# Hash products of twelve rows, four at once, in a kernel of LSH attention and spatial gating

## The chip, the cores and the metric

One core of one Trainium2 chip runs the whole program. The metric is the device time of one execution in microseconds (us), the median of several runs.

## The reference

Two stages, one behind the other. Attention runs over batch 4, heads 8, sequence 768 and head size 64; a query sees only the keys that fall into its own bucket of a random-projection hash of 6 bits. A gated MLP over the sequence follows, with model size 512 and hidden size 1024.

```
q_bits = einsum('bhsd,dk->bhsk', q, proj) > 0        # k_bits the same; 6 bits
mask   = q_bucket[:, :, :, None] == k_bucket[:, :, None, :]
scores = where(mask, q @ k.T / 8, -1e9);  attn = softmax(scores);  x = attn @ v

h = relu(x @ w_in);  u, v = h[..., :512], h[..., 512:]
v_n = (v - mean(v)) / sqrt(var(v) + 1e-6)
out = (u * (einsum('ts,bsd->btd', w_spatial, v_n) + b_spatial)) @ w_out
```

## The kernel before

**The work.** The 32 heads are taken as 16 pairs (`p`), two heads (`e`) in the lower and upper 64 partitions. Each pair has six score steps (`scores`), one for each block of 128 rows. Inputs are float32; each operand is split into a high and a low float16 part, and a product is made of three: `hl` holds the four parts of a pair's q and k. Four passes (`ALL`) make a step's scores in PSUM: three of `hl`, with 64 rows for each head, and a last one of `hk`, the hash rows. A hash row is a bit, scaled so large (`HQ`, `HK`) that a pair of query and key in different buckets falls out of the softmax. Each pass has four products of 384 columns: two halves `c` of the sequence and two heads `e`. Heads lie in different row groups of TensorE (PE), so the two heads of a pass run side by side.

The hash rows (`hash_rows`) are made by PE (`hp`) and VectorE (DVE: `sg`), and moved by eight small DMAs, 12 rows of 384 numbers each, issued by GpSimd (POOL), from `sg` to their place in `hk`. There are two `hk` tiles in turn; those of pair 1 lie in `ws`, which is free that early. Of `hk`, group 1 is the stationary side of a by-query head and group 0 the moving side.

**Two kinds of heads.** Heads 2, 4, 6 and 8 (`KEYS`, in pairs 1 to 4) have their scores laid out with keys on partitions, which needs the maximum of each row ahead of time: `row_max` computes it, `max_row` turns it on PE (`tp`), copies it on DVE (`mt`) and moves it by a DMA of SyncE's queue (SP) into row 63 of the head's `hk`. All other heads go by queries: DVE takes the maximum and the scores out of PSUM (`low`, `ex`), `bias` scales the maximum (`nb`), ScalarE (ACT) takes the exponential and its float16 part (`exp`, `half`: `pp`), DVE or POOL subtracts to get the rest (`rest`), SP turns the result by a DMA transpose (`turn`: `pt`), and PE multiplies it with v (`weighted`: `pv`), four steps later. After four pairs a batch's MLP units become ready: `vps`, `ups`, `sps` and `ops`, groups of three products that PE takes between the steps.

**What sets the order.** The kernel writes every piece of work down as an operation (`op`) with an engine, an estimated length and a rank. `timetable` then plays the engines through and gives each operation a start; where two engines are allowed ("VG") it takes the one that would be first. The program is issued in the order of these starts, and on the chip each engine goes through its own list in that order. The table `LATER` adds to the rank of operations of one name, the paces `T_FIRST` to `T_LAST` say how far apart score steps are planned, `LATE` and `LATE_D` add a margin before PE uses a result, `R_QK` ranks the loads of q and k, `W_FROM` and `W_EVERY` time the weights' loads, and gaps of PE are filled with small warm products (`warm`).

Of the kernel before, what the change touches and what calls it, by code (L numbers as in the profile page):

```python
# [18 lines left out]
P = 128  # L19
D = 64  # L20
NB = 6
# [14 lines left out]
def lsh_attention_spatial_gating(  # L36
# [15 lines left out]
    HS = S // 2  # L52
# [8 lines left out]
    KEYS = WIDE | set()  # L61
    wide = lambda p: any(2 * p + e in WIDE for e in range(2))
    keys = lambda p: [e for e in range(2) if 2 * p + e in KEYS]
    byq = lambda p: [e for e in range(2) if 2 * p + e not in KEYS]
    const = ctx.enter_context(tc.tile_pool(name="const", bufs=1))
    wk = ctx.enter_context(tc.tile_pool(name="wk", bufs=1))
# [8 lines left out]
    AGAIN = {"P": 0.0, "A": 0.11, "V": 0.11, "G": 0.07, "S": 0.0}  # L75
    X = 0.14
    TURN = 1.92
    LATER = {'relu': 0.1, 'first': -0.9, 'bias': -0.3, 'bits': 0.1, 'stats': 0.2, 'half': -0.1, 'copy': 0.6, 'scale': 0.3, 'newton': -0.4, 'turn': 0.1, 'low': 0.6, 'exp': -0.1, 'factor': -0.3}
    ops = []


# [25 lines left out]
    def op(e, d, fn, *after, on=(), rank=4, land=0.0, dma=0.0, need=None, gives=None, alone=False):  # L107
        later = LATER.get(fn.__name__.strip("<>"), 0.0)
        if not isinstance(rank, tuple):
            rank = rank + later  # L110
        elif rank[1]:
            rank = (rank[0] + later, rank[1])
        o = Op(e, d, fn, rank, land, dma)
        o.need, o.gives, o.alone = need, gives, ("V" if alone or "G" in e else "") + ("G" if fn.__name__ != "move" else "")
        wait = [a for a in after if a is not None]
        for h in on:
            assert not h.closed
            if not h.users:
                wait += h.before
            h.users.append(o)  # L120
        for a in {id(a): a for a in wait}.values():
            a.then.append(o)
            o.left += 1
        return o

    def timetable(free, banks):
# [12 lines left out]
        def key(o):  # L139
            return o.rank if isinstance(o.rank, tuple) else (step[0] + (4 if o.rank > 8 else 0), o.rank)  # L140

        def banked(o, e):


            if not o.need:
                return max(o.ready, port[0] + (0.0 if e == port[1] else 0.02)) if e in o.alone else o.ready
            have = sorted(banks[o.need[0]])
            return max(o.ready, have[o.need[1] - 1]) if len(have) >= o.need[1] else None
# [5 lines left out]
        while open_:  # L154
# [12 lines left out]
            for o in came[e]:  # L167
                r = banked(o, e)
                if r is not None and r <= t0 + LOOK and (pick is None or key(o) < key(pick[0])):
                    if not (o.need and o.need[0] in wants and wants[o.need[0]] < key(o)):  # L170
# [38 lines left out]
        for t, n in fill:  # L209
            op("P", 0.07 * n, lambda n=n: warm(n)).start = t  # L210
# [8 lines left out]
    at = {}  # L219
    tags = {}  # L220

    def buf(name, n):
        if name not in tags:
            tags[name] = Buf(n)
        return tags[name]
# [17 lines left out]
    hk = [const.tile([P, 2, S], F16, name=f"hk{i}") for i in range(2)]  # L243
    hkt = lambda p: hk1 if p == 1 else hk[(p + 1) % 2 if p else 0]
    hk1 = flat[1][:, :2 * S].rearrange("p (g s) -> p g s", g=2)
    for i, t in enumerate(hk + [hk1]):
        eng = nc.vector if i < 2 else nc.gpsimd
# [84 lines left out]
    held = {}  # L332

    def load_qk(p, *after):
# [6 lines left out]

        at["qk", p] = op("S", 0.45, go, *after, on=[h], rank=R_QK, dma=2.95)

    def load_v(p, *after):
# [9 lines left out]

        at["v", p] = op("S", 0.5, go, *after, on=[h], rank=R_QK, dma=1.45)

    def urgent(p):

        return NT * p - (8 if keys(p) else 3)

    def hash_rows(p, *after):
        qk, k = held["qk", p], (buf("hk", 2) if p != 1 else buf("hk1", 1)).new()
        held["hk", p] = k
        g0, g1 = buf("sg0", 1).new(), buf("sg1", 2).new()
        hp, sg = [], []

        def go():
            hp.append(bank_m(f"hp{p}"))
            for j in range(4):
                nc.tensor.matmul(  # L370
                    hp[0][32 * j:32 * j + 32, :HS], lhsT=pj,
                    rhs=st["qk", p][:, 1 - j // 2, (j % 2) * HS:(j % 2 + 1) * HS],
                    start=True, stop=True, tile_position=(0, 32 * j))

        def bits():
            sg.append(wk.tile([P, HS], F16, tag="sg0", name=f"sg0_{p}"))
            nc.vector.tensor_scalar(sg[0], hp[0][:, :HS], 0.0, hv[:, 0:1], op0=ALU.is_gt, op1=ALU.subtract)

        def scale():
            sg.append(wk.tile([P, HS], F16, tag="sg1", bufs=2, name=f"sg1_{p}"))  # L380
            nc.vector.tensor_scalar(sg[1], sg[0], hv[:, 1:2], None, op0=ALU.mult)

        t = op("P", 0.8, go, at["qk", p], *after, on=[qk], rank=(urgent(p), 3), need=("m", 1))
        t = op("V", 0.54, bits, t, on=[g0], rank=(urgent(p), 2), gives="m")
        t = op("V", 0.24, scale, t, on=[g0, g1], rank=(urgent(p), 2), alone=True)
        at["hk", p] = []
        for j in range(4):
            for e in range(2):
                q, eng = HQ_FIRST[e] if p == 0 else HQ_REST

                def move(j=j, e=e, eng=eng):
                    eng.dma_start(  # L392
                        out=hkt(p)[D * e:D * e + 2 * NB, 1 - j // 2, (j % 2) * HS:(j % 2 + 1) * HS],
                        in_=sg[1][32 * j + 16 * e:32 * j + 16 * e + 2 * NB, :])
                at["hk", p].append(op(q, 0.53 if q == "G" else 0.75, move, t, on=[g1, k], rank=(urgent(p), 3), land=2.8 if q == "G" else 1.8))

    def split_qk(p, *after):
        qk, h = held["qk", p], (buf("hl", 2) if p != 1 else buf("hl1", 1)).new()
        held["hl", p] = h

        def high():
            if p == 1:
                st["hl", p] = flat[0][:, :4 * S].rearrange("p (g s) -> p g s", g=4)
            else:
                st["hl", p] = wk.tile([P, 4, S], F16, tag="hl", bufs=2, name=f"hl{p}")
            nc.scalar.activation(st["hl", p][:, 1:3], st["qk", p], AF.Copy, scale=SQ)

        t = op("A", 1.39, high, at["qk", p], *after, on=[qk, h], rank=(urgent(p), 4))
        at["hl", p] = [t] + [
            op("V", 0.88, lambda to=to, part=part, frm=frm: nc.vector.scalar_tensor_tensor(  # L410
                out=st["hl", p][:, to], in0=st["qk", p][:, part], scalar=SQ, in1=st["hl", p][:, frm],
                op0=ALU.mult, op1=ALU.subtract), t, on=[qk, h], rank=(urgent(p), 4), alone=True)
            for to, part, frm in ((0, 1, 2), (3, 0, 1))]
# [64 lines left out]
    def sums(ps, p, rows, passes, queries, halves=(0, 1), heads=(0, 1)):  # L478

        for a, (x, y, last) in enumerate(passes):  # L480
            for c in halves:
                cs = slice(c * HS, (c + 1) * HS)
                for e in heads:
                    byq_ = queries or 2 * p + e not in KEYS
                    r = slice(D * e, D * e + D - (last and byq_))
                    src = hkt(p) if last else st["hl", p]
                    l, m = (x, y) if byq_ else (y, x)
                    nc.tensor.matmul(ps[e][:, c - halves[0]], lhsT=src[r, l, rows], rhs=src[r, m, cs],  # L488
                                     start=(a == 0), stop=(a == len(passes) - 1))

    def scores(p, i, g, begin):
        sc = buf("sc", 1).new()

        def go():
            ps = st["sc", p, i] = [ps_sc.tile([P, 2, 512], F32, tag="sc", name=f"sp{p}_{i}_{e}")[:, :, :HS] for e in range(2)]
            sums(ps, p, slice(i * P, (i + 1) * P), ALL, False)

        t = op("P", 1.42, go, *at["hl", p], *at["hk", p], on=[sc, held["hl", p], held["hk", p]], rank=(g, 0))
        t.ready = begin
        at["S now"] = t  # L500
        for e in range(2):
            (by_keys if 2 * p + e in KEYS else by_queries)(p, i, e, g, t, sc)
# [474 lines left out]

    EB, PB, PTB, XTB, VB, UB = 4, 4, 9, 6, 6, 2
    LAG, LAG0, LAGK = 4, 3, 2
    T_FIRST, T_KEYS, T_QUERIES, T_THIRD, T_LAST = 5.0, 5.4, 5.6, 5.95, 5.75  # L980
    START = 6.5
    LOOK = 0
    R_MAX = 0.05
    R_QK = 0.95
    REST, BIAS = (0.88, 1.6), (0.22, 0.25)
    CROSS = {NP - 1}
    R_W = 0.1
    LATE, LATE_D = 0.3, 2.0
    GAP, WARM = 0.5, 5.0
    AHEAD = 1  # L990
    MANY = 36
    W_FROM, W_EVERY = 21.0, 2.0
    HQ_FIRST = (("S", nc.sync), ("A", nc.scalar))
    HQ_REST = ("G", nc.gpsimd)

# [1 line left out]
    load_qk(0)  # L997
    load_v(0)
    hash_rows(0)
    load_qk(1)  # L1000
    split_qk(0)
# [8 lines left out]
    for g in range(STEPS + LAG):  # L1010
        p, i = divmod(g, NT)
        for e in range(2):
            while todo[e] < STEPS and todo[e] + lag[2 * (todo[e] // NT) + e] <= g:
                m, j = divmod(todo[e], NT)
# [97 lines left out]
```

## Time and profile before

| | |
|---|---|
| median of 3 runs | 663.7 us (663.58 to 666.67) |
| profiled execution | 666.77 us, its span 665.0 us |
| granted TensorE clock | 0.99 |
| PE, DVE, ACT, POOL busy | 625.8, 498.4, 476.3, 257.0 us |
| products of `hk` of pairs 5 to 15 | 264, all from 177.8 us on |
| small DMAs `hk<-sg` issued by POOL | 112, 9.0 KB each |
| DMA transposes `pt<-pp` | 168 |

The span is the time from the first to the last instruction. In rows of groups, the numbers behind the bar are busy time, mean length of one in ns, and idle time of the engine before them with what ended it. In rows of the timeline they are start and length in us, engine, line, operation, output and inputs, and a count. Waits are total, number of times, longest. Products overlap, so starts tell more than lengths.

### The profile page before, as it was taken

Reading aid. Unit: us, or ns where it says so; the run is one execution under the profiler, and the core shown is the slowest. Engines: PE = TensorE matmul, PEld = TensorE weight load, DVE = VectorE, ACT = ScalarE, POOL = GpSimd, SP = SyncE. Lnnn points to the kernel's source line nnn. Section 1 sums busy time; section 2 is a strip of 40 time slices with the busy share of each in tenths; the row PEclk is TensorE's granted clock in tenths of the full one; section 3 lists DMA queues with packets and bytes.
Section 4 is the critical chain, followed back from the end, with each engine's and each line's share of the span. In section 5 each row is a group of like instructions: output and inputs, shape, how many; then the busy total and the mean of one; then the engine's idle time right before and its main releaser. Section 6 shows DMA issues by size and latency. Waiting matters only on the chain.

```text
span 665.0 us, 17570 instructions
## 1 busy us (share of the span) xinstructions
PE 625.8 (94%) x7068; PEld 382.8 (58%) x7068; DVE 498.4 (75%) x1019; ACT 476.3 (72%) x802; POOL 257.0 (39%) x318
## 2 busy tenths in 40 slices
PE   5787999998999999999999999999999999999997
PEld 4364767675645655655555566565555665556553
DVE  6787999899898958777867787888877677365250
ACT  2785667867888998777769986787889977463121
POOL 3491624424665757241526345131426541000000
PEclk9797999999999999999999999999999999999999
DMA  5798888894999899999998999899999988210102
GB/s 182 185 183 201 174 170 171 206 219 110 208 189 201 153 193 224 198 184 226 164 232 146 226 141 211 171 221 183 199 215 153 157 140 154 45 47 1 48 1 95
DMA packets 310274, 108.53 MB, mean 163 GB/s; under 512 B 297265, under 2 KB 300337, under 8 KB 310193
## 3 DMA queue, kind: packets, MB, share of 16 engines
q1 hardware_dynamic: 306256, 106.26, 83.4%
q0 software_dynamic: 3840, 1.12, 0.9%
q8 instruction: 55, 0.90, 0.6%
q14 instruction: 27, 0.21, 0.1%
q10 hardware_dynamic: 96, 0.04, 0.0%
HBM read 27.94 MB, written 6.29 MB: 51 GB/s over the span
## 4 chain that ended last, share of the span: by engine, by line
PE 46%; DMA 10%; DVE 8%; issue 5%; ACT 4%; SPq 0%; POOL 0%; DVEq 0%; POOLq 0%; ACTq 0%
DMA pt<-pp 10%; PE sps L742 9%; PE sp L488 9%; PE ops L742 8%; PE pv L645 7%; PE ups L742 6%; PE vps L742 4%; DVE ex L517 3%; PE vpp L742 2%; ACT ex L527 1%; ACT pp L531 1%; DVE hl L410 1%; DVE pp L535 1%; PE upp L742 1%; DVE vr L820 1%
## 5 line engine op out<-in xcount | busy, mean ns | idle before, releaser
L517 DVE TENSOR_SCALAR_CACHE_REDUCE ex<-sp 128x768 f32<-128x768 f32 x168 | 155.7, 951 | 36.8 <-PE sp L488 36.7
L527 ACT ACTIVATE ex<-ex,nb 128x768 f32<-128x768 f32 x168 | 155.4, 932 | 6.6 <-POOL nb L522 4.0
L535 POOL TENSOR_TENSOR pp<-ex,pp 128x768 f16<-128x768 f32 x63 | 104.0, 1657 | 115.4 <-ACT pp L531 85.5
L531 ACT CAST pp<-ex 128x768 f16<-128x768 f32 x168 | 136.1, 825 | 6.2 <-DMA pt<-pp 5.2
L645 PEld LDWEIGHTS <-pt 128*128 128x128 f16 x3024 | 105.6, 97 | 48.8 <-issue 22.4
L535 DVE TENSOR_TENSOR pp<-ex,pp 128x768 f16<-128x768 f32 x105 | 101.2, 979 | 42.9 <-ACT pp L531 41.7
L645 PE MATMUL pv<-vp,pt 128*128 128x65 f16 x3024 | 118.6, 193 | 7.8 <-DMA pt<-pp 6.6
L488 PE MATMUL sp<-hl 64*128 64x384 f16 x1080 | 110.4, 328 | 8.5 <-DVE ex L517 6.2
L742 PE MATMUL sps<-ws,vn 128*128 128x384 f16 x576 | 101.1, 326 | 0.1
L488 PEld LDWEIGHTS <-hl 64*128 64x128 f16 x1116 | 52.8, 95 | 62.4 <-issue 34.9
L742 PEld LDWEIGHTS <-vn 128*128 128x128 f16 x576 | 53.7, 98 | 35.0 <-issue 2.1
L392 POOL DMA_DIRECT2D hk<-sg x112 | 58.0, 525 | 24.2 <-issue 10.3
L742 PE MATMUL ops<-wo,g 128*128 128x512 f16 x288 | 65.9, 379 | 0.4 <-DVE u L906 0.3
L524 ACT ACTIVATE nb<-mr 128x1 f32<-128x1 f32 x125 | 24.5, 197 | 57.8 <-DVE ex L517 57.1
L742 PE MATMUL ups<-xt,wi 128*128 128x384 f16 x348 | 62.4, 326 | 0.0
L742 PE MATMUL vps<-wi,xt 128*128 128x512 f16 x234 | 57.0, 379 | 0.9 <-ACT vr L825 0.7
L488 PE MATMUL sp<-hk 63*128 63x384 f16 (+1 forms) x360 | 48.6, 327 | 2.8 <-DMA hk<-sg 2.3
L742 PEld LDWEIGHTS <-wi 128*128 128x128 f16 x384 | 35.2, 97 | 22.4 <-issue 1.8
L742 PEld LDWEIGHTS <-g 128*128 128x128 f16 x288 | 26.9, 98 | 30.8 <-issue 1.6
L742 PEld LDWEIGHTS <-xt 128*128 128x128 f16 x288 | 25.5, 97 | 28.2 <-issue 3.9
L932 DVE SCALAR_TENSOR_TENSOR sy<-sps,bt 128x384 f32<-128x384 f32 x32 | 17.8, 557 | 31.0 <-PE sps L742 30.6
L940 ACT CAST g<-sy 128x384 f16<-128x384 f32 x32 | 16.3, 508 | 31.4 <-DVE sy L944 30.4
(112 smaller groups left out, 798.2 us busy)
## 6 DMA issues: line engine op xcount, KB each, us to landing
qk<-kq SPq DMA_DIRECT2D x16, 768.0 KB
out<-o SPq DMA_DIRECT2D x24, 256.0 KB
v<-v SPq DMA_DIRECT2D x12, 384.0 KB
pt<-pp SPq DMA_TRANSPOSE x168
raw<-w_in SPq DMA_DIRECT2D x8, 256.0 KB
raws<-w_in SPq DMA_DIRECT2D x8, 256.0 KB
hk<-sg POOLq DMA_DIRECT2D x112, 9.0 KB, 3.8
vf<-v SPq DMA_DIRECT2D x4, 384.0 KB
```

Source lines behind the costliest of these rows:

```text
L392: eng.dma_start(out=hkt(p)[D * e:D * e + 2 * NB, 1 - j // 2, (j % 2) * HS:(j % 2 + 1) * HS], in_=sg[1][32 * j + 16 * e:32 * j + 16 * e + 2 ...
L410: op("V", 0.88, lambda to=to, part=part, frm=frm: nc.vector.scalar_tensor_tensor(out=st["hl", p][:, to], in0=st["qk", p][:, part], scalar= ...
L488: nc.tensor.matmul(ps[e][:, c - halves[0]], lhsT=src[r, l, rows], rhs=src[r, m, cs], start=(a == 0), stop=(a == len(passes) - 1))
L517: nc.vector.tensor_scalar(ex, st["sc", p, i][e], -float(2 ** 28), None, op0=ALU.max, op1=ALU.max, accum_out=st["mx", n][:, i:i + 1])
L524: nc.scalar.activation(nb, mx, AF.Copy, scale=-ISQ)
L527: nc.scalar.activation(st["e32", n, i], st["e32", n, i], AF.Exp, bias=st["nb", n][:, i:i + 1], scale=ISQ)
L531: nc.scalar.copy(st["pp", n, i][:, 0], st["e32", n, i])
L535: eng.tensor_tensor(out=st["pp", n, i][:, 1], in0=st.pop(("e32", n, i)), in1=st["pp", n, i][:, 0], op=ALU.subtract)
L645: nc.tensor.matmul(o, lhsT=l, rhs=m, start=(i == 0 and k == 0), stop=(i == NT - 1 and k == len(todo_) - 1))
L742: nc.tensor.matmul(c[0], lhsT=l(), rhs=r(), start=(j == 0), stop=(j == len(products) - 1))
L932: nc.vector.scalar_tensor_tensor(out=y[0], in0=c[0], scalar=1.0 / (SN * SW), in1=bt[:, hs], op0=ALU.mult, op1=ALU.add)
L940: nc.scalar.copy(gt[h][0][:, d], y[0])
```

## The change

For the pairs behind the last head by keys (`four`, pairs 5 to 15) the hash rows lie in tiles of 32 rows. The moving side's half `c` goes to rows 32c of its head's 64, and the stationary side is written twice, to rows 0 and to rows 32 (`again`: four more DMAs for each pair). The last pass then takes 12 rows at 64e + 32c, a row group of its own for each of its four products; before, it took 63 rows for each head, most of them without a bit. The step's estimated length goes from 1.42 to 1.32. The paces, ranks and margins are other numbers.

```
+    four = lambda p: p > max(KEYS) // 2
-    LATER = {'relu': 0.1, 'first': -0.9, 'bias': -0.3, 'bits': 0.1, 'stats': 0.2, 'half': -0.1, ... 'turn': 0.1, ...}
+    LATER = {'relu': 0.1, 'first': -0.5, 'bias': -0.3, 'bits': 0.1, 'stats': 0.3, 'half': -0.4, ... 'turn': -0.6, 'rest': -0.1}
...
-                def move(j=j, e=e, eng=eng):
+                def move(j=j, e=e, eng=eng, at=32 * (j % 2) if four(p) and j > 1 else 0):
                     eng.dma_start(
-                        out=hkt(p)[D * e:D * e + 2 * NB, 1 - j // 2, (j % 2) * HS:(j % 2 + 1) * HS],
+                        out=hkt(p)[D * e + at:D * e + at + 2 * NB, 1 - j // 2, (j % 2) * HS:(j % 2 + 1) * HS],
                         in_=sg[1][32 * j + 16 * e:32 * j + 16 * e + 2 * NB, :])
...
+                if four(p) and j < 2:
+                    def again(move=move):
+                        move(at=32)
+
+                    at["hk", p].append(op(q, 0.53, again, t, on=[g1, k], rank=(urgent(p), 3), land=2.8))
...
                     r = slice(D * e, D * e + D - (last and byq_))
+                    if last and four(p):
+                        r = slice(D * e + 32 * c, D * e + 32 * c + 2 * NB)
...
-        t = op("P", 1.42, go, ...)
+        t = op("P", 1.32 if four(p) else 1.42, go, ...)
...
-    T_FIRST, T_KEYS, T_QUERIES, T_THIRD, T_LAST = 5.0, 5.4, 5.6, 5.95, 5.75
+    T_FIRST, T_KEYS, T_QUERIES, T_THIRD, T_LAST = 5.0, 5.4, 5.55, 5.75, 5.95
-    R_QK = 0.95
+    R_QK = 1.25
```

`LOOK` goes from 0 to 0.05, `LATE_D` from 2.0 to 2.25, `W_EVERY` from 2.0 to 2.1. Lines of the changed kernel lie one to eight further down. In the built program POOL issues 156 of the small DMAs instead of 112, 23 of the 168 subtractions `pp` have gone from DVE to POOL (DVE 105 to 82, POOL 63 to 86), as have five of `g` and six of `sy`, and there are 444 warm products instead of 436.

The order, at three places. First SP's queue ahead of pair 1; `pt0_4` and `pt1_4` are the transposes of heads 0 and 1 at step 4, `qk3` is the load of pair 3, `raw` are weights, and `ws1<-mt2` is the max row of head 2 (pair 1). Before:

```order
L539 DMA_TRANSPOSE pt0_4_677<-pp0_4_604 128x12x128
L539 DMA_TRANSPOSE pt1_4_713<-pp1_4_654 128x12x128
L340 DMA qk3_760<-kq 128x1536
L292 DMA raw5_784<-w_in 128x256
L619 DMA ws1_80<-mt2_788 1x6x128
L539 DMA_TRANSPOSE pt0_5_814<-pp0_5_735 128x12x128
```

Now:

```order
L547 DMA_TRANSPOSE pt0_4_663<-pp0_4_611 128x12x128
L547 DMA_TRANSPOSE pt1_4_700<-pp1_4_660 128x12x128
L627 DMA ws1_80<-mt2_742 1x6x128
L293 DMA raw5_789<-w_in 128x256
L341 DMA qk3_796<-kq 128x1536
L293 DMA raws_299<-w_in 128x256
L547 DMA_TRANSPOSE pt0_5_875<-pp0_5_846 128x12x128
```

The max row's DMA has moved ahead of the two loads, one more load stands ahead of step 5's transposes.

Second, PE at the turn of that max row (`tp2`). Before, it stands behind head 1's `pv` group of step 3:

```order
L645 MATMUL pv1_483<-vp0_92,pt1_3_630 128x64
L645 LDWEIGHTS pt1_3_630
L645 MATMUL pv1_483<-vp0_92,pt1_3_630 128x65
L612 LDWEIGHTS m16_2_739
L612 MATMUL tp2_767<-ident_71,m16_2_739 6x128
L216 LDWEIGHTS ident_71
```

Now it stands directly behind pair 0's last score step, ahead of head 1's group of step 2:

```order
L496 LDWEIGHTS hk0_81
L496 MATMUL sp0_5_1_641<-hk0_81 128x384
L620 LDWEIGHTS m16_2_638
L620 MATMUL tp2_665<-ident_71,m16_2_638 6x128
L653 LDWEIGHTS pt1_2_544
L653 MATMUL pv1_483<-vp0_92,pt1_2_544 128x65
```

It has moved ahead of three `pv` groups: head 1 of step 2, head 0 and head 1 of step 3.

Third, POOL around the hash rows of pair 12 (`hk1<-sg1_12`); `pp23_1` is the subtraction of head 23 (pair 11) at step 1, `nb24` and `pp25_0` belong to pair 12. Before:

```order
L522 TENSOR_SCALAR nb22_6685<-mr22_6684 128x1
L884 TENSOR_TENSOR vn1_1_6061<-vr1_5_6300,vn1_0_6060 128x512
L392 DMA hk1_82<-sg1_12_6769 12x384 x8
L687 TENSOR_TENSOR xs10_6883<-x20_6846,xs10_6883 128x6x64
L535 TENSOR_TENSOR pp23_1_6888<-ex23_1_6821,pp23_1_6888 128x768
```

Now:

```order
L543 TENSOR_TENSOR pp23_3_7039<-ex23_3_6990,pp23_3_7039 128x768
L955 TENSOR_TENSOR g1_1_0_6897<-sy1_2_0_7029,g1_0_0_6896 128x384
L952 TENSOR_TENSOR sy1_3_0_7125<-sy1_3_0_7125,u1_0_6306 128x384
L393 DMA hk1_82<-sg1_12_7133 12x384 x12
L530 TENSOR_SCALAR nb24_7380<-mr24_7379 128x1
L543 TENSOR_TENSOR pp25_0_7450<-ex25_0_7394,pp25_0_7450 128x768
```

The DMAs have moved from early in pair 11 to directly ahead of pair 12's first step; those of pair 13 stand alike, and those of pairs 5, 6, 7 and 8 shortly ahead of their pair.

More of the change, by code (lines that the diff above doesn't have):

```diff
@@ L77, in lsh_attention_spatial_gating @@
     TURN = 1.92
-    LATER = {'relu': 0.1, 'first': -0.9, 'bias': -0.3, 'bits': 0.1, 'stats': 0.2, 'half': -0.1, 'copy': 0.6, 'scale': 0.3, 'newton': -0.4, 'turn': 0.1, 'low': 0.6, 'exp': -0.1, 'factor': -0.3}
+    LATER = {'relu': 0.1, 'first': -0.5, 'bias': -0.3, 'bits': 0.1, 'stats': 0.3, 'half': -0.4, 'copy': 0.6, 'scale': 0.3, 'newton': -0.4, 'low': 0.6, 'exp': -0.1, 'factor': -0.3, 'turn': -0.6, 'rest': -0.1}
     ops = []
@@ L113, in op @@
         o = Op(e, d, fn, rank, land, dma)
-        o.need, o.gives, o.alone = need, gives, ("V" if alone or "G" in e else "") + ("G" if fn.__name__ != "move" else "")
+        o.need, o.gives, o.alone = need, gives, ("V" if alone or "G" in e else "") + ("G" if fn.__name__ not in ("move", "again") else "")
         wait = [a for a in after if a is not None]
@@ L496, in go @@
             sums(ps, p, slice(i * P, (i + 1) * P), ALL, False)
-        t = op("P", 1.42, go, *at["hl", p], *at["hk", p], on=[sc, held["hl", p], held["hk", p]], rank=(g, 0))
+        t = op("P", 1.32 if four(p) else 1.42, go, *at["hl", p], *at["hk", p], on=[sc, held["hl", p], held["hk", p]], rank=(g, 0))
         t.ready = begin
@@ L979, in lsh_attention_spatial_gating @@
     LAG, LAG0, LAGK = 4, 3, 2
-    T_FIRST, T_KEYS, T_QUERIES, T_THIRD, T_LAST = 5.0, 5.4, 5.6, 5.95, 5.75
+    T_FIRST, T_KEYS, T_QUERIES, T_THIRD, T_LAST = 5.0, 5.4, 5.55, 5.75, 5.95
     START = 6.5
-    LOOK = 0
+    LOOK = 0.05
     R_MAX = 0.05
-    R_QK = 0.95
+    R_QK = 1.25
     REST, BIAS = (0.88, 1.6), (0.22, 0.25)
@@ L987, in lsh_attention_spatial_gating @@
     R_W = 0.1
-    LATE, LATE_D = 0.3, 2.0
+    LATE, LATE_D = 0.3, 2.25
     GAP, WARM = 0.5, 5.0
@@ L991, in lsh_attention_spatial_gating @@
     MANY = 36
-    W_FROM, W_EVERY = 21.0, 2.0
+    W_FROM, W_EVERY = 21.0, 2.1
     HQ_FIRST = (("S", nc.sync), ("A", nc.scalar))
```

## The prediction

> **What bounds the kernel now.** I read the shares of busy time and the slices first, then the stages, then what TensorE (PE) waits for in each of them, and last single steps on the timeline.
>
> ```profile
> span 665.0 us, 17570 instructions
> PE 625.8 (94%) x7068; PEld 382.8 (58%) x7068; DVE 498.4 (75%) x1019; ACT 476.3 (72%) x802; POOL 257.0 (39%) x318
> ...
> PE   5787999998999999999999999999999999999997
> ...
> 0.00:45.00 45.00, 32.67 (x374) 19.94 (x375) 33.10 (x66) 27.30 (x41) 24.94 (x37) 0.92 0.79 179
> 45.00:85.00 40.00, 35.31 (x456) 26.21 (x454) 34.72 (x86) 25.38 (x45) 20.18 (x29) 0.91 0.92 193
> 85.00:178.00 93.00, 84.79 (x1024) 62.50 (x1024) 85.72 (x197) 67.96 (x123) 38.19 (x47) 1.00 0.84 182
> 178.00:320.00 142.00, 136.18 (x1717) 81.23 (x1714) 115.57 (x217) 118.71 (x195) 73.46 (x85) 1.00 1.10 193
> 320.00:457.00 137.00, 135.12 (x1647) 79.29 (x1645) 108.42 (x211) 110.72 (x187) 57.27 (x72) 1.00 1.02 192
> 457.00:557.00 100.00, 98.76 (x1189) 56.97 (x1188) 76.22 (x153) 84.46 (x142) 41.72 (x49) 1.00 1.00 171
> 557.00:665.00 108.00, 103.00 (x677) 56.64 (x671) 44.66 (x92) 41.78 (x77) 1.21 (x2) 1.00 0.17 47
> ```
>
> The columns of a stage are its length, the busy time of PE, weight loads, DVE, ACT and POOL, then PE's clock, the share of the DMA engines and GB/s. The reader is to see two kernels in one. Up to 178 us (pairs 0 to 4, no gating work to fill in with) PE is idle or filled with warm products, and DVE is nearly as busy. From 178 us on, PE has work all the time: 136.18 of 142, 135.12 of 137, 98.76 of 100. What PE waits for, first before and then after 178 us:
>
> ```profile
> PE hp L370 <- DMA qk<-kq: 6.2, 1, 6.2
> PE sp L488 <- DVE ex L517: 4.6, 10, 2.0
> PE sp L488 <- DMA ws<-mt: 3.8, 1, 3.8
> ...
> PE pv L645 <- DMA pt<-pp: 5.5, 9, 1.1
> PE sp L488 <- DVE ex L517: 1.6, 3, 0.6
> PE vps L742 <- ACT vr L825: 0.7, 1, 0.7
> ```
>
> Late waits add up to some 9 us in 487. So behind 178 us the time is the sum of PE's work: what an edit takes off PE there comes off the end, and work that another engine gets costs nothing until PE has to wait for it.
>
> **Four hash products at once.** One score step (L488) of pair 8, with gating products ahead of it and behind:
>
> ```profile
> 301.97 0.65 PE L742 MATMUL sps<-ws,vn 128*128 128x384 f16 x3
> 302.55 1.15 PE L488 MATMUL sp<-hl 64*128 64x384 f16 x12
> 303.54 0.49 PE L488 MATMUL sp<-hk 63*128 63x384 f16 x4
> 303.96 1.15 PE L742 MATMUL sps<-ws,vn 128*128 128x384 f16 x6
> 304.94 0.81 PE L742 MATMUL vps<-wi,xt 128*128 128x512 f16 x3
> ```
>
> Starts are to be read, not lengths, since products are pipelined. Six products of 128 rows take 304.94 - 303.96 = 0.98 us, 0.163 each. Twelve of 64 rows take 303.54 - 302.55 = 0.99, so they run two by two at the same 0.165. But the four hash products, two pairs, take 303.96 - 303.54 = 0.42 and not 0.33, and the three products ahead of the step 0.58 and not 0.49: each passage between 128-row and 64-row products costs 0.09 us. The changed step has one pass of four 12-row products in place of two of two, minus 0.163; but it changes the tile size once more, from 64 rows to 32, plus 0.09. It saves 0.07.
>
> The Trainium skill, TensorEngine Tiling (Array Packing), Key Properties, says that changing the tiling mode drains TensorE, while changing only the tile does not. The trace agrees for 128 to 64 and back (0.09 each); from 64 to 32 no row here shows it. By that rule a step saves 0.07; with no drain between the two it would save 0.163.
>
> How many steps: pairs 5 to 15, which holds in the rows from 177.8 to 558 us:
>
> ```profile
> L488 PE MATMUL sp<-hk 63*128 63x384 f16 x264 | 33.0, 322 | 0.0
> L370 PE MATMUL hp<-qk,hc 128*32 128x384 f32 x80 | 8.5, 498 | 0.0
> L216 PE MATMUL warm<-ident 128*128 128x128 f16 x67 | 4.6, 219 | 0.0
> ```
>
> 264 / 4 = 66 steps, all in the part that PE bounds: 66 x 0.07 = 4.6 us less. The ends are 66 x 0.163 = 10.8 less (no drain) and 66 x 0.09 = 5.9 more (drain paid, and the four run two by two after all). That four tiles do run side by side, the hp row bears out, though for tiles of 32 columns: a record there lasts 498 ns, and eight of them are through in 8.5 / 10 = 0.85 us.
>
> **The max row of pair 1 goes ahead of two loads.** This is in the order of SyncE's queue, not in the words of the change. Before, on SP and on PE:
>
> ```profile
> 44.09 3.32 SPq L539 DMA_TRANSPOSE pt<-pp  x2
> 47.50 0.86 SPq L340 DMA_DIRECT2D qk<-kq  x1
> 48.41 0.45 SPq L292 DMA_DIRECT2D raw<-w_in  x1
> 48.96 0.79 SPq L619 DMA_DIRECT2D ws<-mt  x1
> ...
> 47.46 0.20 DVE L616 COPY mt<-tp 6x128 f16<-6x128 f16 x1
> ...
> 50.84 1.15 PE L488 MATMUL sp<-ws 64*128 64x384 f16 x12
> 55.82 0.82 PE L488 MATMUL sp<-ws 64*128 64x384 f16 x4 [3.84 <-DMA ws<-mt]
> ```
>
> The row was ready at 47.66, was issued at 48.96 behind 768 KB and 256 KB, and came at 55.8, 6.9 us later; PE lost 3.84 on it. Now it stands directly behind the same transposes, so it can go at about 47.7, and has until 51.8, 4.1 us, with no load ahead of it. On PE its transposition stands earlier as well, ahead of three of the `pv` groups that it stood among. Ends: 3.8 less, and nothing (another operand is late as well). DVE was busy 34.72 of 40.00 in this stage, so DVE is late next, at `ex`, and a part comes back: I take 3.0 less. The loads that are passed lose nothing that PE waits for: `qk` of pair 3 is first used one pair later, and the transposes of step 5 stood behind these loads already.
>
> **Forty-four more DMAs on POOL, and hash rows that come late.** Twelve in place of eight issues for each of 11 pairs. Their prices, and pair 5, the only pair behind 178 us whose rows were late before:
>
> ```profile
> L392 POOL DMA_DIRECT2D hk<-sg x80: 500/515/589, 191.4 to 509.2; - x80
> ...
> DMA to landing us min/median/max: 1.7/3.6/6.8
> ...
> L392 POOL DMA_DIRECT2D hk<-sg x8: 500/515/597, 170.4 to 174.0; - x8
> ...
> DMA to landing us min/median/max: 3.2/4.9/5.5
> ...
> 178.82 0.76 PE L488 MATMUL sp<-hk 63*128 63x384 f16 x4
> ```
>
> 44 x 0.52 = 22.9 us of POOL time beside PE. Pair 5's last issue at 174.0 met its use at 178.82 with 0.76 in place of 0.49: 0.27 us lost. In the new order, pairs 5, 6, 7, 8, 12 and 13 have their twelve close ahead of the pair's first step (pair 12's now stand directly before POOL's first bias `nb24` of that pair; before, a whole pair's work lay between). Six times 0.27 is 1.6 us more. Ends: 0, and 6 x 0.8 = 5 (issue as in pair 5, landing at 6.8 in some).
>
> **Moved between engines.** 23 of the subtractions `pp` (L535) go from DVE to POOL, and some twelve of the 384-wide gating ones:
>
> ```profile
> L535 POOL TENSOR_TENSOR pp<-ex,pp 128x768 f16<-128x768 f32 x63 | 104.0, 1657 | 115.4 <-ACT pp L531 85.5
> L535 DVE TENSOR_TENSOR pp<-ex,pp 128x768 f16<-128x768 f32 x105 | 101.2, 979 | 42.9 <-ACT pp L531 41.7
> ```
>
> Each is 1657 - 979 = 0.68 us later, then transposed, then used by `pv` four steps on. POOL gets 23 x 1.66 + 22.9 = 61 us and about 12 for the rest, on 172 us busy of the 379 between 178 and 557: 65%. Covered by the lag, at nothing; if not, `pv` waits longer for `pt`, which is 5.5 us now. Ends: 3 less (transposes now go ahead of loads more often) and 5 more.
>
> **Warm products and pace.** Eight more warm products, 4.6 / 67 = 0.07 each at most: 0.5 more (end: 0, in gaps). The new paces say when a step may be planned, not how long it takes; behind 178 us PE goes on to the next row, so a slower last batch and a faster third move work from one place to another: nothing, within 2 either way for the order up to 178 us.
>
> **The sum.** -4.6 - 3.0 + 1.6 + 0.5 = -5.5. The profiled execution took 666.77 us, of which 665.0 are its span; it would take 661.3. The median of the runs shown is 663.7, 3.1 below that execution, so I forecast 663.7 - 5.5 = 658.2. Runs of this kernel lie 0.46% apart (663.58 to 666.67), so about 0.5%, 3.3 us, is what can be told from no change.
>
> **Rivals.**
> - The four products run two by two (each pair drains its output through a path that carries two). The step becomes 0.09 longer, not 0.07 shorter: +5.9 - 3.0 + 2.1 = +5.0, 668.7, slower. It decides from where the pass of four takes 0.163 + 0.07 = 0.233 us. Against it: the hp row. Chance 0.05.
> - They overlap in part. Halfway between 0.163 and 0.33 the pass takes 0.245, a step is 0.01 longer and all of it 0.8: 0.8 - 3.0 + 2.1 = -0.1, 663.6, no change. Against it: 64-row products pay nothing for running in twos. Chance 0.08. The Trainium skill, TensorE: Matmul & The Clock Gate, Measured speedup vs the span model, gives 3.07 times for four row tiles with K=32, N=512; read as a rate, it makes the pass 4 / 3.07 = 1.3 products long, and by that estimate the sum would be -1.5 - 0.9 = -2.4, 661.3; no run here shows it.
> - No drain from 64 to 32 rows: -10.8 - 0.9 = -11.7, 652.0. For it: the array is split in rows in both; against it: 0.09 at every other passage. Chance 0.08.
> - Transfers bound what lies between 178 and 557 us. The DMA share is 1.00 to 1.10 there, so what PE saves turns into waiting for `pt`, and only the max row is left: 663.7 - 3.0 = 660.7. Against it: PE waits 5.5 us for `pt` in all. Chance 0.11.
> - The hash rows are late at their end of 5 us and some `pt` with them: -4.6 - 3.0 + 5 + 0.5 = -2.1 with their rows alone, and 2 more of `pt`: 663.6, no change. Chance 0.11.
> - What the new order costs up to 178 us, over 6 us: 664 and above. Chance 0.05.
>
> **From these to the numbers.** The forecast's case has 0.52, its own range 654 to 661. Faster by over 0.5% (below 660.4): 0.52 less 0.03, the no-drain case 0.08, and 0.13 of the 0.30 of the overlap's, the transfers' and the late rows' cases, which reach below it: 0.70. Slower (above 667.0): 0.05 two by two, 0.03 of the bad order and 0.03 of late rows: 0.11. Within: the other 0.19. The range leaves out the two-by-two case, the worst orders and half of no drain: 652.3 (-4.6 - 3.8 - 3.0 = -11.4) to 664.0 (late rows with `pt`).
>
> **What would show it.** Right: rows `sp<-hk` of 12 rows, their four starting within some 0.02 us, about 0.25 from the last `hl` product's start to them and 0.25 from them to the next line, so that a step goes from 1.41 to 1.34; no wait for `ws<-mt` at pair 1; PE waits for `hk<-sg` at pair starts of some tenths. Wrong: 0.33 between the first and third product of the four; no 0.09 there; waits of `pv` for `pt` well over 5.5 us, or `hk` waits of a microsecond and more at pairs 5 to 8, 12 and 13; or a stage up to 178 us that ends later than before.

## The result, and the profile after

The changed kernel takes 658.15 us (median of 13 runs, 655.07 to 663.92), the kernel before 665.53 in the runs beside it (13 runs, 663.58 to 670.22): a ratio of 0.9897, interval 0.9867 to 0.9928, or 6.9 us less by the ratio (the two medians lie 7.4 apart). The forecast was 5.5 us less, from a median of 663.7; that its 658.2 was met to a tenth is chance, since the kernel before came out 1.8 us slower in these runs. What follows shows that the total agrees and the sum behind it does not: the tiles took somewhat less off PE than was said, what comes with them takes that back, and the new numbers (paces, ranks and margins) bring the same gain without any tiles.

The profiled execution took 655.07 us, the fastest of the 13. A profile of either kernel can lie some 3 us beside its median, and single profiles are compared below with that in mind. Its page, the parts that answer to those of before:

```profile
span 653.3 us, 17683 instructions
...
PE 615.5 (94%) x7076; PEld 374.4 (57%) x7076; DVE 471.1 (72%) x986; ACT 473.7 (73%) x800; POOL 321.8 (49%) x397
...
PEclk9999999999999999999999999999999999999999
```

POOL has 64.8 us more to do, DVE 27.3 less, PE 10.3 less, and the granted clock is full in all slices (over the 13 executions its mean lies between 0.985 and 1.000). The stages (same columns as before; pair 5 starts at 168.6 us here):

```profile
45.00:85.00 40.00, 36.79 (x457) 26.70 (x454) 38.75 (x97) 31.27 (x58) 19.38 (x27) 1.00 1.00 211
...
175.00:316.00 141.00, 135.45 (x1718) 78.69 (x1715) 104.17 (x211) 117.56 (x195) 97.25 (x112) 1.00 1.09 196
316.00:450.00 134.00, 131.33 (x1632) 76.08 (x1630) 95.76 (x180) 109.12 (x180) 88.24 (x108) 1.00 1.05 193
450.00:545.00 95.00, 91.76 (x1105) 53.25 (x1105) 69.16 (x143) 78.32 (x133) 52.26 (x63) 1.00 0.97 169
```

PE is still busy nearly all the time behind pair 5, though a little less than before: 131.33 of 134 stands where 135.12 of 137 stood. One step late in pair 8 on the timeline, and behind it the group of all hash products of pairs 5 to 15:

```profile
299.08 1.15 PE L496 MATMUL sp<-hl 64*128 64x384 f16 x12
300.16 0.34 PE L496 MATMUL sp<-hk 12*128 12x384 f16 x4
300.44 0.72 PE L653 MATMUL pv<-vp,pt 128*128 128x65 f16 x18
```

```profile
L496 PE MATMUL sp<-hk 12*128 12x384 f16 x264 | 22.6, 331 | 0.0
```

The four products are over in 0.34 us, where one alone lasts 331 ns: they run at once. From the first `hl` product to them it is 1.08, not 0.99, so the passage from 64 to 32 rows costs the 0.09 us that the other passages cost. The Trainium skill (TensorEngine Tiling (Array Packing), Key Properties) says that a change of the tiling mode drains TensorE. This row agrees with it. The step takes 300.44 - 299.08 = 1.36 us instead of 1.41 (the medians of the 66 steps are 1.355 and 1.408). And PE does not wait for the hash rows there: 0.0 us idle before 264 products. In a second profile of the changed kernel, taken below, the four of pair 5 alone are spread, over 0.77 us instead of 0.34.

Where the time lies, by two numbers of each profile: the start of pair 5's first product and the span.

| kernel | up to pair 5 | from pair 5 on |
|---|---|---|
| before | 177.8 | 487.2 |
| changed, first and second profile | 168.6, 173.2 | 484.7, 484.7 |
| new numbers without the tiles, two profiles | 172.7, 169.5 | 485.1, 484.0 |
| changed, second copies left out | 168.8 | 480.8 |
| changed, second copies as fills | 173.1 | 486.0 |
| changed, two products at once | 171.7 | 490.1 |
| before, with another estimate | 177.4 | 493.2 |

The second profile and the last five rows belong to the experiments below. Most of the gain lies ahead of pair 5, where no tile has changed: 9.2 of 11.7 us in the first profile, 4.6 of 7.1 in the second. Behind it the changed kernel stands where the new numbers alone stand. The two profiles of the changed kernel have the same instructions; the second has a stretch at half clock (the 0.50) that the first has not, so the middle column is good to some 4 us:

```profile
122.00:128.80 6.80, 6.77 (x33) 4.35 (x33) 2.74 (x6) 2.61 (x5) 4.49 (x4) 0.50 1.14 233
```

There is a lead in this that no run follows up. Between 15 and 30 us PE's mean clock was 0.77 to 0.89 in the profiles of all four kernels with the old numbers, and below 1.00 in only three of the ten profiles with the new ones. Some of what the new numbers gain ahead of pair 5 may be clock.

### The profile page after: what moved, and what is told of

Read it like the earlier page. It is cut to its first block, busy times and chain, and to the rows that moved or that the text cites. A ratio compares the mean times of both kernels' runs of the same rounds, so it can differ in the third digit from the quotient of the medians.

```text
span 653.3 us, 17683 instructions
## 1 busy us (share of the span) xinstructions
PE 615.5 (94%) x7076; PEld 374.4 (57%) x7076; DVE 471.1 (72%) x986; ACT 473.7 (73%) x800; POOL 321.8 (49%) x397
## 4 chain that ended last, share of the span: by engine, by line
PE 51%; DVE 15%; DMA 11%; ACT 9%; issue 7%; POOL 5%; SPq 1%; DVEq 0%; POOLq 0%; ACTq 0%
PE sps L750 12%; PE sp L496 9%; PE ops L750 9%; PE pv L653 8%; DMA pt<-pp 6%; PE ups L750 5%; DVE ex L525 4%; PE vps L750 3%; ACT pp L539 3%; ACT ex L535 2%; POOL pp L543 2%; DVE pp L543 2%; PE vpp L750 2%; DMA hk<-sg 2%; DVE mx L600 1%
## 5 line engine op out<-in xcount | busy, mean ns | idle before, releaser
L543 POOL TENSOR_TENSOR pp<-ex,pp 128x768 f16<-128x768 f32 x86 | 140.9, 1646 | 74.2 <-ACT pp L539 53.0
L535 ACT ACTIVATE ex<-ex,nb 128x768 f32<-128x768 f32 x168 | 155.3, 932 | 10.5 <-POOL nb L530 7.3
L653 PEld LDWEIGHTS <-pt 128*128 128x128 f16 x3024 | 107.4, 97 | 37.3 <-DMA pt<-pp 13.3
L496 PE MATMUL sp<-hl 64*128 64x384 f16 x1080 | 107.4, 324 | 5.0 <-DVE ex L525 4.7
L393 POOL DMA_DIRECT2D hk<-sg x156 | 79.8, 518 | 50.8 <-issue 15.9
L543 DVE TENSOR_TENSOR pp<-ex,pp 128x768 f16<-128x768 f32 x82 | 79.7, 980 | 34.2 <-ACT pp L539 33.9
L496 PEld LDWEIGHTS <-hl 64*128 64x128 f16 x1116 | 51.1, 94 | 56.8 <-issue 27.5
L496 PE MATMUL sp<-hk 12*128 12x384 f16 (+2 forms) x360 | 37.1, 329 | 4.5 <-DMA hk<-mt 3.5
```

The source lines that it names most:

```text
L393: eng.dma_start(out=hkt(p)[D * e + at:D * e + at + 2 * NB, 1 - j // 2, (j % 2) * HS:(j % 2 + 1) * HS], in_=sg[1][32 * j + 16 * e:32 * j + ...
L535: nc.scalar.activation(st["e32", n, i], st["e32", n, i], AF.Exp, bias=st["nb", n][:, i:i + 1], scale=ISQ)
L543: eng.tensor_tensor(out=st["pp", n, i][:, 1], in0=st.pop(("e32", n, i)), in1=st["pp", n, i][:, 0], op=ALU.subtract)
L653: nc.tensor.matmul(o, lhsT=l, rhs=m, start=(i == 0 and k == 0), stop=(i == NT - 1 and k == len(todo_) - 1))
```

## The experiments

Ratios are to the kernel before, measured beside each on the same chip; the brackets are 95% intervals.

**The tiles undone at the changed kernel's order, first attempt.**

```
-  out=hkt(p)[D * e + at: ...]          at = 32 * (j % 2) or 0;  again: at = 32
+  out=hkt(p)[D * e + at: ...]          at = 0 in all twelve
-  r = slice(D * e + 32 * c, D * e + 32 * c + 2 * NB)
+  r = slice(D * e, D * e + 63)
```

> The changed kernel with its order of instructions and all its DMAs, but the last pass of pairs 5 to 15 takes 63 rows for each head, two products at once, as before (the second copy of the stationary rows is written over the first). The only edit is the shape of 264 products. Theory A (behind 178 us PE's work is the time): a step is 1.41 us again instead of 1.35, 66 x 0.06 = 4.0 us longer than the changed kernel, ratio to the kernel before about 0.996. Rival B (transfers or other engines bound that part, the gain is that of the order alone): the same as the changed kernel, 0.990.

Measured 1.1364 (1.1341 to 1.1386), 756.7 us. Neither theory: the edit brought a wait of its own. POOL's waits, and PE's:

```profile
POOL hk L393 <- DMA hk<-sg: 123.8, 42, 5.8
...
PE sp L496 <- DMA hk<-sg: 43.7, 11, 7.8
```

The second copy went to the same place as the first, so POOL had to wait for the first to land, 42 times, up to 5.8 us each. It says nothing of the tiles, and much of what POOL's waiting costs.

**The same with a free place for the second copy.**

```
-  move(at=32)                       # and the moving side at 32 * (j % 2)
+  move(at=44)                       # and the moving side at 0
-  r = slice(D * e + 32 * c, D * e + 32 * c + 2 * NB)
+  r = slice(D * e, D * e + 44)
```

> The changed kernel with its order, row for row the same on every engine, and all its DMAs; only the last pass of pairs 5 to 15 takes 44 rows of each head (a 64-row tile, two products at once), and the second copy goes to rows 44 to 55, which nothing reads before or after it, so that no DMA waits for another as it did in the first attempt. Theory A (behind pair 5 the time is PE's work): each step 1.41 us in place of 1.35, 66 x 0.06 = 4.0 us more than the changed kernel, ratio to the kernel before 0.9957. Rival B (what the shorter step saves is waited away on transposes): as the changed kernel, 0.9897, with waits of pv for pt that are some microseconds shorter.

Measured 0.9914 (0.9884 to 0.9944). The changed kernel has 0.9897 and, measured again below, 0.9906; so undoing the tiles costs about 1 us by the times, with an interval of some 3 us to either side that does not exclude 3. The single profiles differ by 5.4 us behind pair 5 (490.1 and 484.7), but this one was taken 3 us above its median and the first of the changed kernel's 3 us below. By the timeline (`hl`, then four products over two passes, then `pv`)

```profile
304.73 0.65 PE L496 MATMUL sp<-hl 64*128 64x384 f16 x6
305.22 0.49 PE L496 MATMUL sp<-hk 44*128 44x384 f16 x4
305.64 0.72 PE L653 MATMUL pv<-vp,pt 128*128 128x65 f16 x18
```

the pass takes 0.42 us; the changed kernel's takes 0.28 and a passage of 0.09 ahead of it. That is 0.05, and 66 x 0.05 = 3.3 us. The tiles do save PE's work; how much of the 3.3 comes off the end, between 0 and all, these runs don't settle.

**The 44 second copies left out, same order.**

```
-                        move(at=32)
+                        pass
```

> The changed kernel with the same order and products, but the 44 second copies of the stationary rows are not issued (left out: the second half's hash scores, whose rows stay zero). Theory A (44 issues of 0.52 us lie beside PE's work): as the changed kernel within 1 us, 0.988 to 0.991. Rival B (POOL's time is what takes back the tiles' gain): 3 to 4 us less than the changed kernel, 0.984 to 0.985, with fewer waits of PE for pt.

Measured 0.9826 (0.9800 to 0.9852): 4.7 us under the changed kernel's 0.9897 (5.3 under its second measurement, 0.9906), a little more than Rival B said. The waits behind pair 5, of the changed kernel first and then of this one:

```profile
ACT ex L535 <- POOL nb L530: 7.3, 7, 2.8
...
POOL hk L393 <- PE pv L653: 6.2, 3, 3.3
PE pv L653 <- DMA pt<-pp: 5.8, 8, 1.5
...
POOL hk L393 <- DMA hk<-sg: 4.3, 7, 0.9
```

```profile
POOL hk L393 <- PE pv L653: 5.8, 3, 3.3
...
PE pv L653 <- DMA pt<-pp: 4.8, 7, 1.1
...
ACT ex L535 <- POOL nb L530: 2.4, 4, 0.8
```

Two rows come with the copies. ACT's exponential waits longer for a bias `nb` (7.3 us against 2.4); and POOL's hash DMAs wait for hash DMAs, which the kernel before never did. The longest wait for `nb`, 2.81 us up to 446.3, stands directly behind such a batch in POOL's list:

```profile
438.98 4.55 POOL L393 DMA_DIRECT2D hk<-sg  x9 [2.37 <-DVE sy L940]
444.48 1.52 POOL L393 DMA_DIRECT2D hk<-sg  x3 [0.95 <-DMA hk<-sg]
446.08 0.21 POOL L530 TENSOR_SCALAR nb<-mr 128x1 f32<-128x1 f32 x1
```

PE's own waits behind pair 5 fall from 11.7 to 8.0 us in sum, and the time behind pair 5 from 484.7 to 480.8. Through which of these waits POOL's time reaches PE was not followed step by step.

In the built program POOL's DMAs take eight semaphores in turn, so with twelve the ninth waits until the first has landed:

```
DMA hk1<-sg1_12  (1st)   waits DMASW4, DVE, PE        ...  (9th)   waits DMASW4
DMA hk1<-sg1_12  (2nd)   waits DMASW5, PE             ...  (10th)  waits DMASW5
```

**The copies as fills: POOL's time without the DMAs.**

```
-                        move(at=32)
+                        nc.gpsimd.memset(spare, 0.0)       # spare: 128 x 500 float16
```

> The changed kernel with the same order, but each of the 44 second copies is a fill of a spare tile by POOL that takes about as long as the issue, 0.4 to 0.5 us (left out: the second half's hash scores). POOL's time stays, the DMAs and the waits for them go. Theory A (POOL's ninth to twelfth DMA of a pair waits until the first four have landed, and that holds the work behind them): as with the copies left out, 0.982 to 0.985. Rival B (22.9 us of POOL's time alone): as the changed kernel, 0.988 to 0.991.

The fills (shortest, median, longest in ns), and two waits behind pair 5:

```profile
L400 POOL MEMSET spare<- x44: 518/534/538, 163.9 to 498.7; 128x500 f16 x44
```

```profile
PE pv L654 <- DMA pt<-pp: 8.3, 9, 2.1
...
ACT ex L536 <- POOL nb L531: 4.4, 6, 1.6
```

A fill came to 534 ns, as long as an issue. Measured 0.9879 (0.9844 to 0.9915): 3.5 us above the copies left out, with some 3 to either side, and 1.8 below the changed kernel's second measurement, which the interval does not tell from it. So POOL's time, 44 x 0.52 = 22.9 us of it, has a price by itself, and probably most of the price; the semaphores' turn, which I had expected to be the cause, may have a share. That a fill slows VectorE where an issue would not is not seen: its `ex` take 951 ns each in all three kernels.

**The copies from SyncE's queue, same order, same result.**

```
-                        move(at=32)
+                        nc.sync.dma_start(out=hkt(p)[D * e + 32: ...], in_=sg[1][...])
```

> The changed kernel with the same order and the same result, but the 44 second copies are issued from SyncE's queue at the same places instead of POOL's, so POOL issues eight DMAs a pair as before and none of them waits for one of the same pair. Theory A (POOL's time and its waits for its own DMAs take the tiles' gain back): 3 to 5 us less than the changed kernel, 0.983 to 0.986. Rival B (the copies hurt as transfers, or SP's 44 x 0.73 us delay transposes as much): the same as the changed kernel or slower, 0.989 to 0.995, with longer waits of pv for pt.

PE's longest wait behind pair 5, and ACT's for `nb`:

```profile
PE pv L655 <- DMA pt<-pp: 13.0, 17, 1.9
...
ACT ex L537 <- POOL nb L532: 2.8, 5, 0.8
```

Measured 0.9971 (0.9937 to 1.0006): slower than the changed kernel by 4 to 5 us. ACT's wait for `nb` falls as foreseen, and `pv` waits 13.0 us for transposes instead of 5.8. The transfers are those of the changed kernel; what is new is that they go through the transposes' queue. Rival B holds: that queue was tighter than POOL.

**The new numbers without the tiles, twice.**

```
-    four = lambda p: p > max(KEYS) // 2
+    four = lambda p: False
```

> The changed kernel's paces, ranks and margins, with the hash rows and products of the kernel before (eight DMAs a pair, two products at once); the planner makes an order of its own from them. Theory A (tiles 4 us, the order up to 178 us the other 3): 0.995, with the max row of pair 1 early and no half-clock stretch behind 50 us. Rival B (the numbers alone make it all): 0.990. Rival C (these numbers only help together with the shorter step): 0.999 to 1.004.

Measured 0.9894 (0.9872 to 0.9916), and again:

> The new paces, ranks and margins without the tiles, once more, beside the changed kernel on the same chip. Theory A (the tiles gain 4 us of PE's work and lose as much by their 44 DMAs): within 0.3% of the changed kernel. Rival B (its first time was luck of that chip): 0.994 or above, 3 us and more behind the changed kernel.

Measured 0.9869 (0.9832 to 0.9905), a little beyond Theory A's 0.3% and on the faster side, beside the changed kernel's second time:

> The changed kernel once more, beside the next three on the same chip, for a second profile: its first came from the fastest of 13 runs. Theory A: ratio 0.987 to 0.993, a step of pairs 5 to 15 that takes 1.35 us, no wait for pair 1's max row, and waits of POOL's hash DMAs for earlier hash DMAs of 4 us or more behind 170 us.

Measured 0.9906 (0.9873 to 0.9939), with the waits foreseen behind pair 5:

```profile
ACT ex L535 <- POOL nb L530: 8.6, 7, 3.3
POOL hk L393 <- DMA hk<-sg: 7.7, 9, 1.7
```

With the new numbers, the tiles add nothing: 0.9894 against 0.9897, 0.9869 against 0.9906. The version without them is at least as fast and is the simplest of all, though the difference between the two is within the measurement. Part of the reason stands on PE. The warm products from 177 us on, in the kernel before, in the changed kernel and with the new numbers alone:

```profile
L216 PE MATMUL warm<-ident 128*128 128x128 f16 x87 | 5.8, 219 | 0.0
```

```profile
L217 PE MATMUL warm<-ident 128*128 128x128 f16 x107 | 7.1, 219 | 0.0
```

```profile
L217 PE MATMUL warm<-ident 128*128 128x128 f16 x76 | 5.1, 219 | 0.0
```

The changed kernel runs 31 more of them than the new numbers alone do, 2.0 us of PE's time, against the 3.3 us that its tiles save; PE's waits behind pair 5 are about alike (11.7 and 11.0 us in the changed kernel's two profiles, 10.5 and 10.2 with the numbers alone). A reason that fits, but was not tested: the planner takes 1.32 for a step that lasts 1.36, and fills the time that it believes free.

**The max row of pair 1, from both sides.** The kernel before with that DMA ahead of the two loads, all else in its order; and the changed kernel with it behind them.

```
     timetable(free, banks)
+    sq = sorted([o for o in ops if o.e == "S"], key=lambda o: o.start)
+    m = next(k for k, o in enumerate(sq) if o.rank == 0.05)   # the first max row's DMA
...                                                            # before: row first
+    for k in (1, 2):
+        sq[m - k].start = sq[m].start + 1e-4 * (3 - k)
...                                                            # changed: row last
+    sq[m].start = sq[m + 2].start + 1e-4
```

> The kernel before, with one edit of its order: the DMA of pair 1's max row stands ahead of the load of pair 3's q and k and of one weight load, instead of behind both. Theory A (that row alone holds PE up there): the wait of 3.84 us for it goes, and the half-clock stretch from 54 to 61 us that follows it, so 3 to 5 us less, ratio 0.992 to 0.9955. Rival B (another operand is as late, or the lost time was made up later): within 1 us, 0.9985 to 1.000.

> The changed kernel with one edit of its order: pair 1's max row stands behind the weight load and the load of pair 3's q and k again. Its transposition stays early, so it is issued some 1.5 us later than in the changed kernel and behind 1 MB. Theory A (that row held the kernel before up): PE waits 2 to 4 us for it at pair 1, and the time is 2 to 4 us more, 0.993 to 0.996. Rival B (such a wait is made up for later): within 1 us of the changed kernel.

Row first: 0.9972 (0.9948 to 0.9997), 1.9 us less, between its two theories. Row last: 0.9969 (0.9946 to 0.9993), 4.8 us more than the changed kernel (4.2 more than its second measurement), as Theory A said or a little more. The wait on row last's timeline, the clock in its stages, and the clock in the stages of the kernel before (PE's clock is third from the end):

```profile
48.09 1.13 PE L496 MATMUL sp<-ws 64*128 64x384 f16 x11 [0.51 <-DVE ex L525]
53.58 0.90 PE L496 MATMUL sp<-ws 64*128 64x384 f16 x4 [4.35 <-DMA ws<-mt]
```

```profile
51.00:58.00 7.00, 4.42 (x38) 2.72 (x39) 1.52 (x3) 3.56 (x6) 1.86 (x2) 0.51 0.69 165
```

```profile
45.00:54.00 9.00, 6.26 (x127) 5.18 (x126) 8.08 (x22) 4.18 (x8) 5.42 (x10) 1.00 1.11 253
54.00:61.00 7.00, 5.18 (x37) 3.13 (x37) 3.13 (x7) 3.29 (x6) 0.84 (x1) 0.51 1.03 200
```

With the row in front neither wait nor dip is there; in the kernel before with the row first, DVE is busy 6.14 us of 51 to 58 us, where the kernel before has 3.13 of 7 us in its dip:

```profile
51.00:58.00 7.00, 6.17 (x85) 3.94 (x82) 6.14 (x14) 4.43 (x9) 0.75 (x1) 1.00 1.23 239
```

So one DMA of 1.5 KB, two places further back in SP's queue, costs 2 to 5 us: PE stands, its clock goes to half for 6.8 us, and DVE and ACT, which PE feeds, have less to do meanwhile.

**The tiles under the old numbers.**

```
LATER, T_*, LOOK, R_QK, LATE_D, W_EVERY: as before;  the rest as changed
```

> The tiles of 32 rows, the four more DMAs a pair and the step's shorter estimate, with the paces, ranks and margins of the kernel before; the planner makes an order of its own. Theory A (work of PE off the end): 66 x 0.06 = 4.0 us less, 0.994, with the wait for pair 1's max row still there. Rival B (POOL's 44 more DMAs under the old numbers make hash rows or transposes late): 0.998 to 1.003, with waits of PE for hk of a microsecond and more.

Measured 1.0306 (1.0283 to 1.0329), worse than either theory. PE's waits behind pair 5:

```profile
PE pv L653 <- DMA pt<-pp: 19.2, 17, 2.8
PE pv L653 <- DVE x L682: 1.3, 1, 1.3
```

No wait for `hk` there, but 19.2 us for transposes. From the page:

```profile
PE 633.7 (92%) x7157; PEld 385.5 (56%) x7157; DVE 465.4 (68%) x974; ACT 475.6 (69%) x804; POOL 344.3 (50%) x405
```

PE has more to do than before, not less: the planner has put in 89 more warm products, all of them behind pair 5 (176 there instead of 87). POOL has 87 us more. To see how much of it the planner makes:

**A number that only the planner sees.**

```
-        t = op("P", 1.42, go, ...)
+        t = op("P", 1.32 if p > 4 else 1.42, go, ...)          # kernel before, the step still takes 1.41
```

> The kernel before, with one number changed that costs nothing on the chip: the planner is told 1.32 for a step of pairs 5 to 15, and the step still takes 1.41. It makes another order. Theory A (a set of numbers fits one set of costs, and any other input makes a worse order): 1.01 to 1.03, with more warm products and longer waits of pv for pt, as with the tiles under the old numbers. Rival B (the old numbers' order is robust, and the tiles with their 44 DMAs themselves cost the 3%): within 0.3% of the kernel before.

Measured 1.0135 (1.0110 to 1.0160): 9 us more, as Theory A said. No operation that the result needs is longer, but the program is another one. Its warm products from 177 us on, and PE's longest wait behind pair 5:

```profile
L216 PE MATMUL warm<-ident 128*128 128x128 f16 x171 | 11.3, 219 | 0.0
```

```profile
PE pv L645 <- DMA pt<-pp: 6.5, 11, 1.7
```

There are 84 more warm products than in the kernel before, 5.5 us of PE's time, and 25 more subtractions `pp` on POOL. In the profiles the part behind pair 5 is 6.0 us longer (493.2 against 487.2), so nearly all of that is warm products, which fits the 66 x 0.1 = 6.6 us that the planner wrongly believes free. Of the tiles' 20 us under the old numbers an amount of this size is explained, since they come with as many warm products. The other large part, 19.2 us of waits for transposes instead of 5.5, the control does not show (6.5); whether the 44 DMAs or their order make those waits is open.

## Why the prediction was right in its total, and wrong in its sum

- **What bounds the kernel.** Right: PE's work behind pair 5, chains of waits ahead of it. The products taken off do show in a step (1.41 to 1.36). The rival that transfers bound this part is not borne out: PE waits 5.8 and 4.7 us for `pt` there, and 5.5 before.
- **Four hash products, -4.6.** The mechanism held in each part: side by side, one passage more, hardly any overlap lost. A step saves 0.05, not 0.07, so 3.3 us of work; the times of the two-at-once kernel put what reaches the end at about 1, with 3 not excluded. The rivals "two by two", "overlap in part" and "no drain" fall by the rows of a step: four in 0.34 us, and the next line 0.28 after their first, of which 0.09 are the passage. That leaves 0.19 for the pass, where 0.163 was said. The Trainium skill gives 3.07 times for four row tiles (TensorE: Matmul & The Clock Gate, Measured speedup vs the span model). Read as a rate it would make the pass 0.21, an estimate from that figure, and the row is only a little below it; but the four lasting 0.34 us where one lasts 0.33 speaks against four in a row at such a rate. (In "overlap in part", 66 x 0.01 is 0.7 us and not 0.8; nothing hangs on it.)
- **The max row, -3.0.** Right in place, and in size within the measurement: -1.9 alone in the kernel before, 4.2 to 4.8 lost when it is put back. What the step left out is the half clock behind the wait.
- **44 DMAs, hash rows late, +1.6.** Wrong. In the first profile no product of pairs 5 to 15 waited for them, and in the second only pair 5's were spread, by 0.4 us. They were planned close, and still in time.
- **"Covered by the lag, at nothing".** This is the step that failed. 22.9 us more on POOL, 65% busy by my count (64% measured: 237.75 of 370 in the three stages after), were put down as hidden, because `pv` comes four steps later. But POOL also makes the bias `nb` that ACT waits for, and POOL's list is in order: the DMAs stand ahead of it. Left out, they give 4.7 us back; its upper end, 5 more, was named and not taken. That they cost this is shown; that it goes by way of `nb` is argued from the waits.
- **Warm products, +0.5.** Too small. There are eight more in all, but 20 more behind pair 5, where PE has no time to spare: 1.3 us (7.1 against 5.8).
- **"Nothing, within 2 either way" for the numbers.** Wrong by the most. They make 0.987 to 0.989 by themselves, 7 to 9 us; the max row's 2 to 5 are among them, the rest was not found in the order that I looked at. By single profiles they are worth 2 to 3 us from pair 5 on, and 5 to 8 ahead of it.

The two large errors have opposite signs: POOL's time costs 4.7 us that the sum had at nothing, and the numbers gain some 4 to 6 us that it had at nothing. That the sum came out within 1.4 us is luck. What was not tried: which of the numbers does what else, one edit of the order at a time ahead of pair 5 besides the max row, and the tiles with an estimate that fits their step.

## What to carry to other kernels

An engine that is two thirds busy on average need not hide a burst: 6 us of issues can stand ahead of a 0.2 us operation that another engine waits for, however long the lag of what was meant to be moved. In a kernel whose order comes from a planner, compare an edit at a fixed order, and change the planner's estimate alone as a control; here that control moved the time by 1.35%, more than the change itself is worth. Then count what the planner has added: an estimate 0.1 us too short for 66 steps had come back as 84 warm products. And look at the queue for small transfers behind large ones: 1.5 KB behind 1 MB was worth about as much as 264 products.

## What the runs showed of the hardware that was not expected

- PE's waits of 3.84 and 4.35 us for the max row were followed by 6.8 us at half clock (0.51 over 54 to 61 and 51 to 58 us). The tiles under the old numbers and the estimate alone had that wait too, 4.0 and 4.1 us, and 3.4 us at half clock behind it (0.51 over 55.5 to 59.0, 0.50 over 57.6 to 61.0). Without the wait the clock stayed at 1.00 there. The Trainium skill (TensorE: Matmul & The Clock Gate, Why this matters for your kernels) warns of idle gaps over some 3 us between bursts of products. These four agree. A long wait is not the only way to half clock, though: the changed kernel's second profile had 6.8 us of it (0.50 over 122.0 to 128.8), and no wait of PE between 105 and 130 us was longer than 1.4.
- Four tiles of 12 rows with 384 columns lasted 0.34 us together; a change from 64-row to 32-row tiles costs the same 0.09 us as one from 64 to 128.
- Where a DMA had to follow another to the same place, POOL's list stood until that one had landed: 123.8 us over 42 waits, and the kernel took some 90 us longer than the kernel before.
